# Attention, low-rank mix and feed-forward on one core: own buffers for the raw W2 chunks, W2 remainders on VectorE, and measured durations in the planner

## The chip, the core and the metric

The kernel runs on one core of one Trainium2 chip. The core has five instruction queues: TensorE (PE in the profile, its weight loads PEld), VectorE (DVE), ScalarE (ACT), GpSimd (POOL) and SyncE (SP, which only issues DMAs here). Each takes its instructions in order, and an instruction that waits for a semaphore holds all that stand behind it on the same engine. The metric is the device time of one execution in microseconds, the median of several runs.

## The reference

Eight batches, eight heads, 576 positions, 64 channels a head. Two attentions are added (one over positions averaged by four, one over a window of seven positions), then a low-rank mix along the sequence (rank 32), then a feed-forward net from 512 to 2048 and back. Cut to what matters:

```python
q_d, k_d, v_d = (x.reshape(B, H, 144, 4, D).mean(axis=3) for x in (q, k, v))
out_up = np.repeat(sm_attn(q_d, k_d, v_d), 4, axis=2)
mask = np.abs(pos[:, None] - pos[None, :]) < 4
scores = np.where(mask, scale * q @ k.transpose(0, 1, 3, 2), -1e9)
x = out_up + softmax(scores) @ v             # then heads side by side: (8, 576, 512)
u = x + (x.transpose(0, 2, 1) @ U @ V).transpose(0, 2, 1)
out = u + np.maximum(u @ w_ch1, 0.0) @ w_ch2  # 512x2048, 2048x512
```

U, V and the two weight matrices arrive as 64-bit floats.

## The kernel before

**Feed-forward.** It takes most of the time of TensorE. u is kept transposed, channels on the partitions. A step is one batch (8), one half t of its positions (2 x 288) and one block fc of 128 of the 2048 hidden channels (16): 256 steps. Every product is made from operands that are split into a high part (H) and a remainder (L), as three matmuls: high by high, high by remainder, remainder by high. So F1 of a step (line 891) is 4 x 3 matmuls of 128x128 by 288 into a PSUM buffer ps_h, of which there are two. ScalarE writes hH, its rectified high part (line 898), VectorE the remainder hL (line 899). F2 of the same step (line 914) comes three steps later (LAG = 3): four groups of three matmuls into four accumulators acc, which run over the 16 blocks of a half. At the end of a half GpSimd adds uH and uL (line 924), VectorE adds that to each accumulator (line 928), and SyncE stores the result (line 931). Steps are counted from 0; step 32 is the first of batch 1.

**Attention and mix.** They work on two heads at a time, a head pair hp (four to a batch). Batch 0 goes through a way of its own (the "early" functions), with buffers in a pool named early. Batches 1 to 7 go through late_global, late_scores, local_attn and mix_part: q and k are loaded (gq, gT, line 570), GpSimd averages them (gh, smq, smk) and v (vr, vs, lines 511 and 513); TensorE makes both kinds of scores (ps_b, lines 718 and 725), ScalarE copies the local ones (se), SyncE stores them to a scratch in DRAM (s_s, line 751) and loads them back in another layout (sc, line 757). The global attention ends with ps_t (line 540), ps_a (line 553), od (VectorE, line 557) and four stores up_s (line 562). In the local attention, GpSimd multiplies the window of v with the weights (Pt, line 798, five pieces to a pair, three buffers), VectorE sums them (acc, line 803), SyncE stores the sum (x_s, line 805). It is loaded back as xL and Y (lines 821 to 832) for the mix: GpSimd takes the remainder of xL (line 839), TensorE multiplies with U (ps_hu, line 847) and V (ps_u, line 862), VectorE adds (xT, line 865), ScalarE writes uH (line 868) and GpSimd uL (line 870). Then the pair is ready for F1. The attention of batch b + 1 is planned beside the feed-forward of batch b.

**Weights.** W1 and W2 come as 16 chunks each of 512 KB (lines 390 and 398) into raw buffers. Three slots, which later serve as the products Pt of the local attention, hold all raw chunks in turn. A chunk is converted (convert, lines 336 to 351): ScalarE brings out the upper bits (upper, line 339), VectorE joins them with the lower ones (c, line 342), ScalarE writes the high part (W1H or W2H, line 346), GpSimd the remainder (W1L or W2L, line 349). W2H and W2L lie where the early pool was, so that their writes wait for the key "late", which the last operation of batch 0's attention sets; the loads of W2 do not wait for it. F1 waits for it as well from step 3 on.

**What sets the order.** Nothing is written out by hand. Every operation is put into a Plan with its engine, an estimate of its duration, what it reads and writes, and a priority. Plan.run (line 104) is a list scheduler that simulates the five engines with these estimates, and the order that comes out is the program's. The helpers dve, act and pool_tt (lines 270 to 277) turn a number of elements and a base or a rate into a duration. The matmuls of the feed-forward have the lowest priority (FILL) and so fill what the attention leaves free; hH, hL and the output adds have the highest (FIRST). So a changed estimate can move any instruction on any engine.

The three places where the estimates enter:

```python
return op(DVE, ((n / 2 if two_x else n) + 65) / 960.0, fn, r, w, prio)
return op(ACT, n / 1200.0 + base, fn, r, w, prio)
return op(POOL, 0.147 + n * ns / 1000.0, fn, r, w, prio, after)
```

## Time and profile before

| what | us |
|---|---|
| median of three runs | 980.32 |
| the three runs | 980.32, 982.18, 973.27 |
| the profiled execution | 982.36 |
| its span in the profile | 980.6 |

The profile is of one execution. Its page gives the busy time of each engine; further views give it by stretches of time, the chain of waits that ended last, the timeline of each engine, and groups of instructions by line. In a row of a timeline stand the start, the duration (both in us), the engine, the line of the kernel, the operation, its output and inputs, and in brackets how long the engine was idle ahead of it and what ended that. The mean granted clock of TensorE is 0.975 of full speed. By the page, 120.19 MB were moved by DMA, at a mean of 123 GB/s.

### The profile page before, as it was taken

The numbers are of one execution on the slowest core, as the hardware profiler recorded it, in microseconds if no ns is written. First come the engines' busy times: TensorE is split into PE (matmuls) and PEld (weight loads), VectorE is DVE, ScalarE is ACT, GpSimd is POOL, SyncE is SP. The second block draws the span as 40 slices with busy tenths as digits, with TensorE's granted clock in tenths as the row PEclk, the third lists the DMA queues.
The fourth block names the chain that finished last, engine by engine and source line by source line (L and its number), as shares of the span: only waits on it lengthen the run. The fifth ranks groups of instructions, "written<-read, shape, count | busy, mean of one in ns | idle before, by whom it ended". The sixth has DMA issues, their size and how long they took to land.

```text
span 980.6 us, 26568 instructions
## 1 busy us (share of the span) xinstructions
PE 928.4 (95%) x10712; PEld 907.5 (93%) x10712; DVE 475.3 (48%) x948; ACT 391.0 (40%) x1239; POOL 555.2 (57%) x591
## 2 busy tenths in 40 slices
PE   5878999859999999999999999999999999999998
PEld 4667989849999999999999999999999999999998
DVE  4554576544455655543555555544555544532122
ACT  3677653433344333443344334443344344221111
POOL 6786677766665746574656656565566646431010
PEclk9788999959999999999999999999999999999999
DMA  9858855655555455546555455545536454310000
GB/s 249 214 192 220 237 150 138 145 124 129 126 139 120 111 120 110 147 88 149 124 123 126 106 126 119 136 104 143 127 97 143 110 124 84 88 37 25 1 25 25
DMA packets 222930, 120.19 MB, mean 123 GB/s; under 512 B 174724, under 2 KB 199128, under 8 KB 222808
## 3 DMA queue, kind: packets, MB, share of 16 engines
q1 hardware_dynamic: 222808, 118.51, 49.7%
q8 instruction: 84, 1.38, 0.6%
q14 instruction: 38, 0.31, 0.1%
HBM read 87.60 MB, written 30.86 MB: 121 GB/s over the span
## 4 chain that ended last, share of the span: by engine, by line
PE 81%; DVE 7%; DMA 3%; issue 3%; ACT 3%; POOL 2%; SPq 1%; DVEq 0%; POOLq 0%; ACTq 0%
PE ps_h L891 35%; PE acc L914 34%; PE ps_a L553 3%; DVE acc L803 3%; PE ps_b L718 2%; PE ps_hu L847 1%; PE ps_t L540 1%; PE ps_b L725 1%; DVE o L928 1%; DVE c L342 1%; DMA kd<-in_kT 1%; POOL W2L L349 1%; PE ps_u L862 1%; PE ps_hu L666 1%; DMA w2r<-in_W 1%
## 5 line engine op out<-in xcount | busy, mean ns | idle before, releaser
L891 PE MATMUL ps_h<-uH,W1H 128*128 128x288 f32 x1024 | 298.2, 291 | 5.8 <-DVE hL L899 5.8
L914 PE MATMUL acc<-hH,W2H 128*128 128x288 f32 x1024 | 300.6, 294 | 2.5 <-ACT W2H L346 2.5
L891 PE MATMUL ps_h<-uL,W1H 128*128 128x288 f32 x1024 | 294.8, 288 | 0.0
L891 PE MATMUL ps_h<-uH,W1L 128*128 128x288 f32 x1024 | 294.7, 288 | 0.0
L914 PE MATMUL acc<-hH,W2L 128*128 128x288 f32 x1024 | 294.2, 287 | 0.5 <-POOL W2L L349 0.5
L914 PE MATMUL acc<-hL,W2H 128*128 128x288 f32 x1024 | 294.0, 287 | 0.0
L798 POOL TENSOR_TENSOR Pt<-vl,at 128x896 f32<-128x896 f32 (+1 forms) x140 | 227.0, 1690 | 108.1 <-DVE acc L803 53.4
L899 DVE SCALAR_TENSOR_TENSOR hL<-ps_h,hH 128x288 fp32r<-128x288 f32 x256 | 116.5, 455 | 331.7 <-ACT hH L898 328.2
L898 ACT ACTIVATE hH<-ps_h 128x288 fp32r<-128x288 f32 x256 | 104.7, 409 | 343.8 <-PE ps_h L891 340.7
L891 PEld LDWEIGHTS ps_h<-uH,W1H 128*128 128x128 f32 x1024 | 195.6, 191 | 8.7 <-DVE hL L899 7.6
L914 PEld LDWEIGHTS acc<-hH,W2H 128*128 128x128 f32 x1024 | 194.6, 190 | 3.0 <-ACT W2H L346 2.6
L891 PEld LDWEIGHTS ps_h<-uL,W1H 128*128 128x128 f32 x1024 | 195.6, 191 | 0.0
L914 PEld LDWEIGHTS acc<-hH,W2L 128*128 128x128 f32 x1024 | 194.6, 190 | 0.9 <-POOL W2L L349 0.9
L891 PEld LDWEIGHTS ps_h<-uH,W1L 128*128 128x128 f32 x1024 | 195.4, 191 | 0.0
L914 PEld LDWEIGHTS acc<-hL,W2H 128*128 128x128 f32 x1024 | 194.7, 190 | 0.0
L803 DVE TENSOR_REDUCE acc<-Pt 128x128 f32<-128x1024 f32 (+1 forms) x140 | 151.5, 1104 | 2.6 <-POOL Pt L798 1.5
L839 POOL TENSOR_TENSOR xL<-xL,xH 116x640 fp32r<-116x640 f32 x28 | 43.3, 1545 | 105.8 <-ACT xH L838 93.4
L743 ACT ACTIVATE se<-ps_b 96x114 f32<-96x114 f32 x112 | 39.8, 355 | 77.3 <-PE ps_b L718 56.2
L924 POOL TENSOR_TENSOR o<-uH,uL 128x288 f32<-128x288 f32 x48 | 36.9, 797 | 50.4 <-DMA out_t<-o 50.4
L511 POOL TENSOR_TENSOR vr<-vr 72x256 f32<-72x256 f32 x56 | 40.8, 729 | 36.5 <-DMA vr<-in_v 36.5
L792 ACT ACTIVATE Pt<-ul 128x128 f32<-128x128 f32 (+1 forms) x140 | 48.5, 422 | 25.3 <-DVE acc L803 21.5
L870 POOL TENSOR_TENSOR uL<-xT,uH 128x288 fp32r<-128x288 f32 x56 | 43.7, 801 | 22.0 <-ACT uH L868 22.0
(130 smaller groups left out, 1043.7 us busy)
## 6 DMA issues: line engine op xcount, KB each, us to landing
vl<-in_vp SPq DMA_DIRECT2D x56, 240.0 KB
w1r<-in_W SPq DMA_DIRECT2D x16, 511.8 KB
w2r<-in_W SPq DMA_DIRECT2D x16, 511.8 KB
gT<-in_kT SPq DMA_DIRECT2D x28, 291.0 KB
gq<-in_qT SPq DMA_DIRECT2D x28, 288.0 KB
vr<-in_v SPq DMA_DIRECT2D x56, 144.0 KB
up_s<-od SPq DMA_DIRECT2D x112, 72.0 KB
ul<-up_s SPq DMA_DIRECT2D x28, 288.0 KB
```

Of the source, the lines that this page charges most:

```text
L511: pool_tt(256, lambda x=x: nc.gpsimd.tensor_tensor(out=x()[:, :, 0:2, :], in0=x()[:, :, 0:2, :], in1=x()[:, :, 2:4, :], op=ALU.add), [x], ...
L743: act(n * KL, lambda p=ps[hh], se=se, n=n, rows=rows: nc.scalar.activation(se()[rows, 0:n].rearrange("p r k -> p (r k)"), p()[rows, 0:n * ...
L792: act(n * D, lambda n=n, ps=ps, Pt=Pt: nc.scalar.activation(Pt()[:, :n, :, 7], ul()[:, ps, :], AF.Copy), [ul], [(Pt, 1)], prio, 0.16)
L798: nc.gpsimd.tensor_tensor(out=Pt()[:, :n, :, 0:7].rearrange("p s d o -> p o s d"), in0=win, in1=at()[:, ps, :].rearrange("p s o -> p o s") ...
L803: dve(8.5 * n * D, lambda n=n, ps=ps, Pt=Pt: nc.vector.tensor_reduce(out=acc()[:, ps, :], in_=Pt()[:, :n], axis=AX.X, op=ALU.add), [(Pt, 0 ...
L839: pool_tt(640, lambda: nc.gpsimd.tensor_tensor(out=xL(), in0=xL().bitcast(F32), in1=xH().bitcast(F32), op=ALU.subtract), [xL, xH], [xL], prio)
L870: pool_tt(TN, lambda uH=uH, uL=uL, uf=uf: nc.gpsimd.tensor_tensor(out=uL()[:, hp, :], in0=uf(), in1=uH()[:, hp, :].bitcast(F32), op=ALU.su ...
L891: nc.tensor.matmul(ps()[:, :TN], w[:, dc, fs], turns(u()[:, dc, :]), start=(n == 0), stop=(n == 3 * NDC - 1))
L898: last_h[i] = act(TN, lambda: nc.scalar.activation(hH(), ps()[:, :TN], AF.Relu), [ps], [hH], FIRST, 0.05)
L899: dve(TN, lambda: nc.vector.scalar_tensor_tensor(hL(), ps()[:, :TN], 0.0, hH().bitcast(F32), op0=ALU.max, op1=ALU.subtract), [ps, hH], [hL ...
L914: nc.tensor.matmul(ac[e]()[:, :TN], W2[w][:, fc, es], turns(hx()), start=(fc == 0 and n == 0), stop=(fc == NFC - 1 and n == 2))
L924: pool_tt(TN, lambda e=e, o1=o1: nc.gpsimd.tensor_tensor(out=o1()[:, :TN].bitcast(F32), in0=uH()[:, e, :].bitcast(F32), in1=uL()[:, e, :]. ...
```

## The change

It has three parts.

1. Raw chunks 0 to 11 of W2 get four buffers of their own, in a pool "raws" that is laid into the space of the early pool once batch 0's attention has ended. Chunks 12 to 15 stay in the three shared slots. The converted chunks 0 to 11 lie in a tile W2a beside the raw buffers; when all of them are converted, the raw buffers are given up and chunks 12 to 15 are converted into a tile W2b in their place. High part and remainder lie side by side in both. So the load of chunks 0 to 11 now waits for "late"; the load of chunk f of the last four waits for the high part of chunk f - 4, and its conversion for a key "last".

2. The remainder of every W2 chunk is taken by VectorE instead of GpSimd (16 instructions of 128x512). W1, U and V stay on GpSimd.

3. Some forty estimates of durations are replaced.

No instruction is added or removed, and none but the 16 remainders changes its engine. The diff's core, with some of the estimates:

```diff
+class Later:
+    def __init__(self):
+        self.pool = None
+
+    def tile(self, *a, **k):
+        return self.pool.tile(*a, **k)
...
+    NFA = 12
...
+    first = tc.tile_pool(name="raws", bufs=1)
+    raws = Later()
+
     def late_pool():
-        if not W2:
-            early.__exit__(None, None, None)
-            w2p = ctx.enter_context(tc.tile_pool(name="w2p", bufs=1))
-            W2["H"] = w2p.tile([128, NFC, DM], F32R, name="W2H")
-            W2["L"] = w2p.tile([128, NFC, DM], F32R, name="W2L")
-        return W2
+        early.__exit__(None, None, None)
+        w2p = ctx.enter_context(tc.tile_pool(name="w2a", bufs=1))
+        W2["a"] = w2p.tile([128, NFA, 2, DM], F32R, name="W2a")
+        raws.pool = first.__enter__()
+
+    def last_pool():
+        first.__exit__(None, None, None)
+        w2p = ctx.enter_context(tc.tile_pool(name="w2b", bufs=1))
+        W2["b"] = w2p.tile([128, NFC - NFA, 2, DM], F32R, name="W2b")
+
+    def w2(f, i):
+        return W2["a"][:, f, i] if f < NFA else W2["b"][:, f - NFA, i]
...
-    def convert(raw, pp, n, hi_out, lo_out, a, wkey, name, prio, gate=(), l0=0):
+    def convert(raw, pp, n, hi_out, lo_out, a, wkey, name, prio, gate=(), l0=0, rest=POOL):
...
-        dve(1.2 * n, lambda: nc.vector.scalar_tensor_tensor(
+        dve(1.75 * n, lambda: nc.vector.scalar_tensor_tensor(
...
-        pool_tt(1.0 * n, lambda: nc.gpsimd.tensor_tensor(
+        eng, put = (nc.vector, dve) if rest == DVE else (nc.gpsimd, pool_tt)
+        put(1.25 * n if rest == DVE else 1.08 * n, lambda: eng.tensor_tensor(
             out=lo_out(), in0=ta()[l0:], in1=hi_out()[l0:].bitcast(F32), op=ALU.subtract),
...
     def load_w2(f, prio):
-        raw = raw_buf("w2r")
-        dma(lambda: nc.sync.dma_start(out=shifted(raw, 128, CN), in_=w2.bitcast(I16)[f * 128:(f + 1) * 128, 1:]),
-            [], [raw], prio, 525)
-        convert(raw, 128, CN, lambda: W2["H"][:, f, :].unsqueeze(1),
-                lambda: W2["L"][:, f, :].unsqueeze(1), 1, f"W2_{f}", "c2", prio, ["late"])
-
+        key, gate = f"W2_{f}", "late" if f < NFA else "last"
+        own = f < NFA
+        raw = buf(raws, [128, 2 * CN], I32, "w2r", None, 4) if own else raw_buf("w2r")
+        dma(lambda: nc.sync.dma_start(out=shifted(raw, 128, CN), in_=w2_in.bitcast(I16)[f * 128:(f + 1) * 128, 1:]),
+            [gate] if own else [f"W2_{f - 4}H"] if f >= NFA else [], [raw], prio, 525)
+        convert(raw, 128, CN, lambda: w2(f, 0).unsqueeze(1), lambda: w2(f, 1).unsqueeze(1), 1, key, "c2", prio,
+                [gate], rest=DVE)
...
-            pool_tt(7 * n * D, prod, [vl, at], [(Pt, 0)], prio, 1.75)
+            pool_tt(7 * n * D, prod, [vl, at], [(Pt, 0)], prio, 1.9)
...
-        last_h[i] = act(TN, lambda: nc.scalar.activation(hH(), ps()[:, :TN], AF.Relu), [ps], [hH], FIRST, 0.05)
-        dve(TN, lambda: nc.vector.scalar_tensor_tensor(
+        last_h[i] = act(TN, lambda: nc.scalar.activation(hH(), ps()[:, :TN], AF.Relu), [ps], [hH], FIRST, 0.17)
+        dve(TN + 82, lambda: nc.vector.scalar_tensor_tensor(
...
+    begun = len(plan.ops)
     for f in range(NFC):
+        if f == NFA:
+            plan.op(DVE, 0.0, lambda: last_pool(), [], ["last"], 27, after=plan.ops[begun:], lat=0.0)
         load_w2(f, W2P + W2S * f)
```

How the order moves is shown at three places. Line numbers of the changed kernel are 18 to 20 higher (390 becomes 409, 891 becomes 911, 914 becomes 934). A number behind x says how many like instructions follow one another.

SyncE's issues around the end of batch 0's attention; w1r and w2r are raw chunks, gq and gT the q and k of batch 1's first head pair, s_s its stores of scores. Before:

```order
L390 DMA w1r<-in_W 128x2047 x3
L509 DMA vr<-in_v 72x2x256
L390 DMA w1r<-in_W 128x2047 x3
L570 DMA gq<-in_qT 128x576
L570 DMA gT<-in_kT 128x582
L751 DMA s_s<-se 32x3x38 x3
L751 DMA s_s<-se 32x9x38
L751 DMA s_s<-se 32x3x38 x3
L751 DMA s_s<-se 32x9x38
L390 DMA w1r<-in_W 128x2047
L398 DMA w2r<-in_W 128x2047
```

The same place now:

```order
L409 DMA w1r<-in_W 128x2047 x8
L590 DMA gq<-in_qT 128x576
L419 DMA w2r<-in_W 128x2047 x4
L771 DMA s_s<-se 32x3x38 x3
L771 DMA s_s<-se 32x9x38
L771 DMA s_s<-se 32x3x38 x3
L771 DMA s_s<-se 32x9x38
L590 DMA gT<-in_kT 128x582
L419 DMA w2r<-in_W 128x2047 x3
```

The last chunk of W1 and the first four of W2 now stand ahead of the eight stores of scores; gT stands behind them.

TensorE at the end of batch 0, from the last F2 group (acc) of step 31 on; ps_hu and ps_u belong to the mix of a head pair, the others to attention. Before:

```order
L914 MATMUL acc_2372<-hH,W2L 128x288
L847 MATMUL ps_hu<-xH,Ust 64x128 x5
L847 MATMUL ps_hu<-xL,Ust 64x128 x5
L862 MATMUL ps_u<-Vst,stk 128x288 x2
L553 MATMUL ps_a<-vs,E 72x64 x8
L725 MATMUL ps_b<-smk,smq 32x144 x4
L725 MATMUL ps_b<-smk,smq 8x144 x2
L718 MATMUL ps_b<-gT,gq 32x38 x30
L725 MATMUL ps_b<-smk,smq 32x144 x4
L725 MATMUL ps_b<-smk,smq 8x144 x2
L718 MATMUL ps_b<-gT,gq 32x38 x6
L540 MATMUL ps_t<-ident_sb,E 72x72 x8
```

Behind these stand, before and now, ps_hu and ps_u of head pair 3 and then F1 of step 32. Now:

```order
L934 MATMUL acc_2340<-hH,W2b 128x288
L573 MATMUL ps_a<-vs,E 72x64 x8
L745 MATMUL ps_b<-smk,smq 32x144 x4
L745 MATMUL ps_b<-smk,smq 8x144 x2
L738 MATMUL ps_b<-gT,gq 32x38 x30
L745 MATMUL ps_b<-smk,smq 32x144 x4
L745 MATMUL ps_b<-smk,smq 8x144 x2
L738 MATMUL ps_b<-gT,gq 32x38 x6
L560 MATMUL ps_t<-ident_sb,E 72x72 x8
L867 MATMUL ps_hu<-xH,Ust 64x128 x5
L867 MATMUL ps_hu<-xL,Ust 64x128 x5
L882 MATMUL ps_u<-Vst,stk 128x288 x2
```

ps_hu and ps_u of head pair 2 have gone from here: ps_hu now stands ahead of F2 of step 28, ps_u ahead of F2 of step 29. Those of pair 0 moved from F2 of step 21 to that of step 17, those of pair 1 from behind F1 of step 29 to behind F2 of step 23. On SyncE, at this place, gq, gT and four stores of scores have come ahead of the load of xL, and on VectorE the four output adds of line 928 stand ahead of the last three sums acc of head pair 3.

TensorE at the start of a later batch (step 96), where the third F1 group of the batch follows the second. Before:

```order
L891 MATMUL ps_h<-uH,W1L 128x288
L891 MATMUL ps_h<-uH,W1H 128x288
L891 MATMUL ps_h<-uL,W1H 128x288
L891 MATMUL ps_h<-uH,W1L 128x288
L553 MATMUL ps_a<-vs,E 72x64 x8
```

Now:

```order
L911 MATMUL ps_h<-uH,W1L 128x288
L573 MATMUL ps_a<-vs,E 72x64 x8
L911 MATMUL ps_h<-uH,W1H 128x288
L911 MATMUL ps_h<-uL,W1H 128x288
L911 MATMUL ps_h<-uH,W1L 128x288
```

ps_a has moved from behind the third group to between the second and the third. At the start of batch 2 (step 64), ps_a and a head pair's scores stand ahead of the first and the second group in the same way. Just ahead of these places, ps_u of head pair 3 has moved: before, it stands ahead of F2 of the third step from the end of the batch, now among the four groups of F2 of the last step. At the last batch (step 224) nothing stands between the first three F1 groups, before and now.

More of the change, by code (lines that the diff above doesn't have):

```diff
@@ L675, in early_mix @@
             [ph, (stk, 0)], [(stk, 1)], prio)
-        act(128, lambda: nc.scalar.activation(stk()[3 * R:4 * R], ph()[:R, :2 * D], AF.Copy), [ph], [(stk, 2)], prio, 0.1)
+        act(128, lambda: nc.scalar.activation(stk()[3 * R:4 * R], ph()[:R, :2 * D], AF.Copy), [ph], [(stk, 2)], prio, 0.16)
         for t in range(NT):
@@ L738, in mm @@
                 dense(3, r)
[L739 removed]
+        op(PE, 1.38, mm, [qr, kr, sq, sk, "early_hu"], ps, prio)
         for hh in range(2):
@@ L850, in mix_part @@
         stk = buf(mix, [128, 2, D], F32R, "stk", bufs=2)
-        act(128, lambda: nc.scalar.activation(stk()[0:2 * R], pv(), AF.Copy), [ph], [(stk, 0)], prio, 0.05)
+        act(128, lambda: nc.scalar.activation(stk()[0:2 * R], pv(), AF.Copy), [ph], [(stk, 0)], prio, 0.17)
         dve(128, lambda: nc.vector.tensor_tensor(
@@ L854, in mix_part @@
             [ph, (stk, 0)], [(stk, 1)], prio)
-        act(128, lambda: nc.scalar.activation(stk()[3 * R:4 * R], pv()[0:R], AF.Copy), [ph], [(stk, 2)], prio, 0.05)
+        act(128, lambda: nc.scalar.activation(stk()[3 * R:4 * R], pv()[0:R], AF.Copy), [ph], [(stk, 2)], prio, 0.17)
         for t in range(NT):
```

81 lines of the change are left out of this document (40 added, 41 removed).

## The prediction, made before the changed kernel was run

> **What bounds the kernel now.** I read the first part of the page, then the busy time by stretches of time, then the chain of waits where those show a hole, then the timelines of single engines there.
>
> From the page, the busy time of the engines (share of the span, instructions):
>
> ```profile
> PE 928.4 (95%) x10712; PEld 907.5 (93%) x10712; DVE 475.3 (48%) x948; ACT 391.0 (40%) x1239; POOL 555.2 (57%) x591
> ```
>
> TensorE is the bound on average: 980.6 us of span less 928.4 leaves 52.2 us that can be won without taking matmuls away. Where they lie is told by TensorE's busy time by stretches: first one whole batch (111.5 us, the next four are alike), then all engines in 25 us stretches.
>
> ```profile
> 328.50:440.00 111.50, 110.58 (x1299) 1.00 0.52 122
> ```
> ```profile
> 75.00:100.00 25.00, 20.45 (x246) 19.17 (x245) 12.07 (x26) 18.52 (x52) 17.09 (x19) 0.86 0.85 218
> ...
> 175.00:200.00 25.00, 19.46 (x163) 18.82 (x163) 15.47 (x30) 8.05 (x23) 20.17 (x21) 0.97 0.49 111
> 200.00:225.00 25.00, 16.20 (x176) 14.40 (x177) 11.74 (x21) 9.71 (x32) 16.59 (x19) 0.55 0.60 135
> 225.00:250.00 25.00, 25.00 (x305) 24.79 (x305) 11.01 (x22) 10.02 (x34) 15.29 (x17) 1.00 0.52 117
> ```
>
> (Columns: length, busy PE, PEld, DVE, ACT, POOL, granted clock, DMA share, GB/s.) From 225 us on TensorE is never idle for long: 0.94 us in each batch. The holes are before that: 4.55 us at 75 to 100 and 5.54 + 8.80 = 14.3 us at 175 to 225, where the clock also falls to 0.55. The first is the start of the second matmul, the other the change from batch 0 to batch 1. So the change can act at three places: the start, that one boundary, and the 0.94 us per batch.
>
> **The start (chunks of W2).** TensorE's row where the second matmul first runs, SyncE's issues ahead of it, then the conversions on VectorE and GpSimd, grouped by line:
>
> ```profile
> 86.67 0.61 PE L914 MATMUL acc<-hH,W2H 128*128 128x288 f32 x1 [2.47 <-ACT W2H L346]
> ```
> ```profile
> 63.51 6.42 SPq L390 DMA_DIRECT2D w1r<-in_W  x3
> 72.04 0.33 SPq L570 DMA_DIRECT2D gq<-in_qT  x1
> ...
> 72.90 4.33 SPq L751 DMA_DIRECT2D s_s<-se  x8
> 77.33 0.40 SPq L390 DMA_DIRECT2D w1r<-in_W  x1
> 78.48 0.35 SPq L398 DMA_DIRECT2D w2r<-in_W  x1
> ```
> ```profile
> L342 DVE SCALAR_TENSOR_TENSOR c<-w1r,upper x16: 653/867/2364, 25.5 to 82.6; 128x512 int32<-128x512 int32 x16
> L342 DVE SCALAR_TENSOR_TENSOR c<-w2r,upper x16: 675/961/1230, 84.8 to 133.8; 128x512 int32<-128x512 int32 x16
> ```
> ```profile
> L349 POOL TENSOR_TENSOR W2L<-c,W2H x16: 1270/1278/1714, 86.7 to 137.5; 128x512 fp32r<-128x512 f32 x16
> ```
> ```profile
> 70.96 0.80 POOL L699 TENSOR_TENSOR uL<-uf,uH 128x288 fp32r<-128x288 f32 x1
> 71.71 1.28 POOL L349 TENSOR_TENSOR W1L<-c,W1H 128x512 fp32r<-128x512 f32 x1
> ```
> ```profile
> 71.33 2.22 DVE L342 SCALAR_TENSOR_TENSOR c<-w1r,upper 128x512 int32<-128x512 int32 x1 [1.39 <-issue]
> ```
>
> Step by step. The first W2 load is issued at 78.48 and its product starts at 86.67: 8.19 us from issue to use. In the old order it stands behind eight stores of scores (4.33 us) and the sixteenth W1 load. In the new one all W1 loads and one gq load come first, four W2 loads follow, the stores come after. Two things can hold the new load: the gate "late", open when the last work of batch 0's attention ends (uL at 70.96 + 0.80 = 71.76), so with gq's 0.33 an issue at about 72.4; or the sixteenth W1 load, which needs the slot of the thirteenth chunk, whose c ends at 71.33 + 2.22 = 73.55, then 0.40 for itself and 0.33 for gq: 74.3. Adding 8.19 gives 80.6 or 82.5; I take the middle, 81.6, which is 5 us earlier. Ends: 6.1 us of gain; against it, three more W1 conversions now stand ahead of the first hL on VectorE, 3 x 0.867 = 2.6 us of loss if nothing covers them. What covers them now is the time until the first F1 product is there; without it the 2.6 us falls due.
>
> Moved behind the four W2 loads (about 4 x 0.35 = 1.4 us, more if the slots are late) are the stores of scores of batch 1's first head pair. I cost that at nothing on the path, since F1 of batch 1, for which that chain works, is 145 us away; without that cover it is 1.4 us.
>
> Remainders on VectorE: no row of before has this one there. The nearest is c, same 128x512 and also two inputs in SBUF: 0.675 alone, 0.961 in the middle, 1.230 at worst. I take 0.961: 16 x 0.961 = 15.4 us more for VectorE, hidden in a stretch where it is half idle (12.07 of 25 us busy), and 16 x 1.278 = 20.4 us less for GpSimd. On the path to F2.0 lies one of them: 0.3 us won, contained in the middle I took. If VectorE were blocked for as long as c was at worst, 2.364, a remainder would cost 1.1 us against 1.278 and F2.0 came at 82.7.
>
> The trace shows VectorE's c stretched from 0.653 to 2.364 us when GpSimd works beside it. The Trainium skill, "SBUF — State Buffer", section "SBUF: two separate sides", has a rule that speaks against this move: a VectorE operation with two inputs in SBUF and a GpSimd operation that reads SBUF take the shared ports as an exclusive lock, and the one that comes second waits for the whole of the other. By it each remainder on VectorE gives back up to 0.675 us of the 1.278 that GpSimd is spared, so GpSimd would win 16 x 0.603 = 9.6 us rather than 20.4, and F2.0 would wait for one more GpSimd operation of 1.28 us: a start term of -3.7 in place of -5, a sum 1.3 us higher. The stretched rows agree with the rule; how often the two meet in the new order no row tells.
>
> **The boundary from batch 0 to batch 1.** The chain of waits there (three of its pieces), TensorE's timeline, then SyncE's and VectorE's:
>
> ```profile
> 188.39 4.42 PE acc L914 x36
> ...
> 208.36 0.47 SPq L821
> ...
> 217.34 6.92 PE ps_h L891 x36
> ```
> ```profile
> 192.64 0.47 PE L847 MATMUL ps_hu<-xH,Ust 116*64 116x128 f32 x5
> ...
> 213.07 0.80 PE L847 MATMUL ps_hu<-xH,Ust 116*64 116x128 f32 x5 [1.47 <-ACT xH L838]
> ```
> ```profile
> 201.91 0.33 SPq L805 DMA_DIRECT2D x_s<-acc  x1
> 203.13 0.34 SPq L509 DMA_DIRECT2D vr<-in_v  x1
> 204.87 3.38 SPq L562 DMA_DIRECT2D up_s<-od  x4
> 208.36 0.47 SPq L821 DMA_DIRECT2D xL<-x_s  x1
> ...
> 211.49 1.86 SPq L751 DMA_DIRECT2D s_s<-se  x4
> ...
> 215.85 0.40 SPq L570 DMA_DIRECT2D gq<-in_qT  x1
> 216.30 0.42 SPq L570 DMA_DIRECT2D gT<-in_kT  x1
> ```
> ```profile
> 193.54 0.64 DVE L928 TENSOR_TENSOR upper<-acc,upper 128x288 f32<-128x288 f32 x1
> ...
> 198.22 1.22 DVE L803 TENSOR_REDUCE acc<-Pt 128x128 f32<-128x1024 f32 x1
> ```
>
> Call the end of batch 0's half with step 31 T: 188.39 + 4.42 = 192.8. F1 of batch 1 (step 32) starts at 217.34, T + 24.5; it waits for head pair 3, whose sums are stored at 201.91 (T + 9.1), queue behind up_s, and from the reload at 208.36 take 8.98 us to F1. In the new order the sums (hu) of head pair 2 no longer stand in this hole but four steps earlier. VectorE has four output adds and three sums left behind T: 4 x 0.64 + 3 x 1.22 = 6.2, the store is issued at T + 6.2. Ahead of the reload on SyncE then stand the store 0.33, vr 0.34, up_s 3.38, gq and gT 0.82 and four stores of scores 1.86, 6.7 together: reload at T + 12.9, F1 at T + 21.9. That is 2.6 us sooner. This is an edit that removes and adds: 9.1 - 6.2 = 2.9 us won ahead of the store, the scores' stores and gq, gT added on SyncE. Bounds: if three of the four adds are done before T, as the old order has them, 1.9 us more (-4.5); if the chain is set by the distance of head pairs alone, -7.4 (below); on the other side the new items of SyncE on top of the old times, +2.7.
>
> **The later boundaries.** TensorE's waits between 300 and 900 us, and from the chain a filler's length:
>
> ```profile
> PE ps_h L891 <- DVE hL L899: 4.7, 5, 1.0
> ```
> ```profile
> 225.74 1.03 PE ps_a L553 x16
> ```
>
> Five times, at a batch's start, the third F1 group waits 0.94 us for a buffer that hL still reads. In the new order ps_a (1.03 us) stands between the second and third group: five waits filled, 5 x 0.94 = -4.7 us. Its price is that the matmuls of head pair 3 (ps_u) move from 4 us ahead of the batch's first F1 to right ahead of it, 1.1 us of matmuls between. How long the path from ps_u to uL takes, TensorE's and GpSimd's rows for pair 2 of batch 1 show:
>
> ```profile
> 185.03 0.43 PE L862 MATMUL ps_u<-Vst,stk 128*128 128x288 f32 x2
> ```
> ```profile
> 186.37 0.80 POOL L870 TENSOR_TENSOR uL<-xT,uH 128x288 fp32r<-128x288 f32 x1 [2.33 <-ACT uH L868]
> ```
>
> That is 187.17 - 185.03 = 2.14 us. Covered are 1.1 us of matmuls and three quarters of the first F1 group (1.1 of 1.47 us), since it reads head pair 3 last: 2.2. So I cost the move at nothing; what comes later than that TensorE waits for, at each of six boundaries.
>
> Sum, on the profiled execution (982.36 us): -5 - 2.6 - 4.7 = -12.3, so 970.1. The median of the runs is 980.32, 2.04 lower: 968.
>
> **Rivals.**
> A, as summed: 968, own range 962 (start -6.1, boundary -7.4, and 4.7) to 975 (start nothing).
> B, batch 1's attention chain sets the time of F1.32, whenever F2 starts: the waits between 175 and 225 are all for that chain, so an earlier start only lengthens them. The sums of pairs 0 and 1, too, stand four or five steps earlier among TensorE's instructions, which run in order: if the chain isn't earlier by as much, TensorE waits there, and has the wait of the boundary sooner. Then both first terms vanish and 980.32 - 4.7 = 975.6 is left. For it: TensorE is idle 14.3 us there while GpSimd is 20.17 of 25 us busy; against it: GpSimd loses 20.4 us of work before that.
> C, the boundary follows the distance of head pairs: hu of pair 2 at 192.64 and of pair 3 at 213.07 are 20.4 us apart. Pair 2's now stands 7.6 us ahead of T (five groups of 1.47 and a ps_u of 0.26), so pair 3's falls at T + 12.8 and F1, 4.27 us after it, at T + 17.1: -7.4 in place of -2.6, 963. For it: those distances are the chain's own; against: the queue of SyncE just counted.
> D, slower: head pair 3 arrives just too late at every boundary. The place is GpSimd's uL between two products Pt, rows of the page:
>
> ```profile
> L798 POOL TENSOR_TENSOR Pt<-vl,at 128x896 f32<-128x896 f32 (+1 forms) x140 | 227.0, 1690 | 108.1 <-DVE acc L803 53.4
> L511 POOL TENSOR_TENSOR vr<-vr 72x256 f32<-72x256 f32 x56 | 40.8, 729 | 36.5 <-DMA vr<-in_v 36.5
> ```
>
> With two Pt and one vr ahead of it, 2 x 1.69 + 0.73 = 4.1 us, on top of the 2.14 us that the 2.2 us just cover, each of six boundaries loses 4.0: +24, which makes 968 into 992. It decides from 2 us of lateness on (6 x 2 = 12, the whole gain). For it: the order has no slack left there; against: GpSimd is a third idle late in the run (57% busy).
>
> **How the numbers follow.** About 1%, 9.8 us, is what a measurement of this kernel can tell from no change. A 0.45, B 0.25, C 0.15, D 0.15. The time is A's. The range leaves out D and little else: low 958 (C with the best start is 962; the 2.5 us that the first three F1 groups lose to the low clock, 6.92 against 3 x 1.47, and the 1.9 of the adds take it there), high 983 (B with the boundary 2.7 us worse, and one Pt late at some boundaries). Faster by over 1% is below 970.5: C whole and about 0.28 of A's 0.45: 0.43. Within 1%: the rest of A and B: 0.42. Slower: D, 0.15.
>
> **What would show it.** Start right: the first second-matmul row at 80 to 83 us; wrong: at 86 or later. Boundary right: F1 of batch 1 some 22 us after T, and the clock still low there; C: 17; B: F1 at 217 whatever T is. Later right: 110.5 us a batch in place of 111.4, and no wait for hL; D: waits of F1 for uL at six boundaries. Remainders: 0.7 to 1.2 us on VectorE, and GpSimd busy some 20 us less. What would make all of it wrong is a new wait on VectorE between 80 and 140 us, where conversions, remainders and hL now share one queue.

## The result, and the profile after

The changed kernel takes 990.74 us, the median of four runs (989.33 to 992.37). The kernel before took 976.80 us beside it (four runs, 972.62 to 982.18). The ratio is 1.0142, 95% interval 1.0097 to 1.0186: slower by some 14 us, where 12 us less was forecast.

The profiled executions are closer: 989.67 us (span 987.8) after, 982.36 us (span 980.6) before. A second profile of the kernel before, taken in the study, gave 982.74 us and the same times of its steps within 0.5 us from step 17 on, while the medians of its timed runs lay between 976.80 and 980.38. So a profile of the kernel before lies 2 to 6 us above the medians of its timed runs; why, no run told. Below, ratios come from timed runs, and the profiles are used for places.

The page of the changed kernel, busy time by engine:

```profile
PE 933.2 (94%) x10712; PEld 912.3 (92%) x10712; DVE 482.1 (49%) x964; ACT 387.6 (39%) x1239; POOL 538.2 (54%) x575
```

GpSimd lost 17.0 us and VectorE gained 6.8. The 16 remainders take 14.2 us on VectorE, while its conversions c became 4.7 us shorter and its operations ms and at of the attention 3.1. Twelve of the remainders (shortest, middle and longest in ns):

```profile
L368 DVE TENSOR_TENSOR W2a<-c,W2a x12: 675/684/2094, 82.4 to 113.4; 128x512 fp32r<-128x512 f32 x12
```

TensorE is busy 4.8 us longer with the same 10712 matmuls, at a mean granted clock of 0.965 instead of 0.975.

Where the time went is told best by a clock made of steps: the start of hH on ScalarE, minus the same in the kernel before (first profile), for the changed kernel and for some of the experiments below. A number that grows from one column to the next is time lost there, or work of the attention that one order has there and the other elsewhere.

| kernel | step 4 | 17 | 18 | 32 | 63 | 64 | 128 | 223 | 224 | 255 |
|---|---|---|---|---|---|---|---|---|---|---|
| before, us | 90.83 | 142.09 | 145.03 | 220.41 | 325.42 | 332.62 | 555.42 | 876.78 | 883.64 | 971.78 |
| changed | -5.6 | -7.5 | +1.3 | +1.2 | +1.5 | +8.3 | +6.5 | +5.6 | +7.7 | +7.7 |
| durations alone | -8.0 | -8.7 | -10.1 | -5.0 | -6.1 | -2.4 | -3.4 | -4.2 | -2.1 | -2.1 |
| raw buffers alone | -0.8 | -4.2 | -1.8 | -0.9 | -1.7 | +2.0 | +2.0 | +2.0 | +2.0 | +2.0 |
| changed, ms later | -6.8 | -9.4 | -6.0 | -3.3 | -3.4 | +3.5 | +1.7 | +0.9 | +3.1 | +3.1 |
| changed, slack x 0.75 | -6.5 | -5.8 | -5.7 | -2.6 | +1.4 | -3.2 | -4.6 | -7.7 | -11.6 | -8.6 |

Read along the second row, the changed kernel wins 7.5 us by step 17, loses 8.8 in the one step from 17 to 18, holds that over the boundary to batch 1, loses 6.8 from step 63 to 64 (5.0 of it still there at step 128), gains back about 0.4 at the start of each later batch (it stands at +5.7 at step 192), and loses 2.1 at step 224. The three losses are three places. They turn the -7.5 us of step 17 into +7.7 at step 255; the timed runs differ by 14 us, and the rest of that has no place in these profiles.

**Start.** TensorE's timeline of the changed kernel, the first row of the second matmul:

```profile
82.28 0.36 PE L934 MATMUL acc<-hH,W2a 128*128 128x288 f32 x1
```

It ran at 86.67 before: 4.4 us sooner. SyncE issues the four W2 loads behind gq, as the order said; below are GpSimd's last uL of batch 0:

```profile
73.74 0.33 SPq L590 DMA_DIRECT2D gq<-in_qT  x1
74.27 2.94 SPq L419 DMA_DIRECT2D w2r<-in_W  x4
```
```profile
72.23 2.02 POOL L719 TENSOR_TENSOR uL<-uf,uH 128x288 fp32r<-128x288 f32 x2
```

They end at 72.23 + 2.02 = 74.25, and that opens the gate "late": the loads go out at 74.27.

**Step 17 to 18.** TensorE's one large wait there, then VectorE, then GpSimd at the same time:

```profile
141.24 0.46 PE L745 MATMUL ps_b<-smk,smq 64*32 64x144 f32 x5 [3.81 <-DVE od L577]
```
```profile
135.37 5.49 DVE L789 SCALAR_TENSOR_TENSOR ms<-sc,mask_sb 128x63 f32<-128x63 f32 x1
140.78 0.41 DVE L577 TENSOR_TENSOR od<-ps_a,ri 72x256 f32<-72x256 f32 x1
```
```profile
135.02 0.73 POOL L531 TENSOR_TENSOR vr<-vr 72x256 f32<-72x256 f32 x1
135.71 5.15 POOL L818 TENSOR_TENSOR Pt<-vl,at 128x896 f32<-128x896 f32 x3
```

ms has 63 elements a partition. The other 27 of this trace took 0.22 us in the middle and 0.55 at most; here it takes 5.49, until 140.86, which is the end of GpSimd's third Pt (135.71 + 5.15). od stands behind it on VectorE, and the scores on TensorE wait for od. The clock falls with the wait (0.86 in this stretch; columns as in the prediction):

```profile
125.00:150.00 25.00, 20.69 (x243) 19.88 (x242) 20.75 (x26) 11.09 (x37) 19.12 (x19) 0.86 0.59 146
...
175.00:200.00 25.00, 22.80 (x278) 21.80 (x276) 12.80 (x23) 10.17 (x34) 18.78 (x22) 0.95 0.51 124
200.00:225.00 25.00, 12.48 (x143) 10.98 (x143) 10.20 (x22) 9.20 (x32) 15.12 (x16) 0.50 0.54 123
```

**Boundary to batch 1.** The last two rows are its hole: 2.20 + 12.52 = 14.7 us idle, against 14.3 before. TensorE's rows there:

```profile
195.14 0.29 PE L934 MATMUL acc<-hH,W2b 128*128 128x288 f32 x1
...
206.55 1.41 PE L560 MATMUL ps_t<-ident_sb,E 72*72 72x72 f32 x8 [3.40 <-ACT E L546]
213.33 0.79 PE L867 MATMUL ps_hu<-xH,Ust 116*64 116x128 f32 x5 [5.37 <-ACT xH L858]
...
217.40 0.44 PE L911 MATMUL ps_h<-uH,W1H 128*128 128x288 f32 x1
```

The end T of batch 0 is 195.14 + 0.29 = 195.4, and F1 of batch 1 follows at T + 22.0. Before, T was 192.8 and the same row stood at 217.13, T + 24.3 (the chain gives 217.34). Two rows of SyncE, the store of pair 3's sums and its reload, give the pieces:

```profile
199.90 0.33 SPq L825 DMA_DIRECT2D x_s<-acc  x1
207.52 0.47 SPq L841 DMA_DIRECT2D xL<-x_s  x1
```

The store goes out at T + 4.5, the reload at T + 12.1, and F1 comes 9.9 us after it.

**Step 64.** TensorE, and what VectorE does while TensorE waits for stk:

```profile
331.65 0.29 PE L934 MATMUL acc<-hH,W2b 128*128 128x288 f32 x1
334.22 0.82 PE L882 MATMUL ps_u<-Vst,stk 128*128 128x288 f32 x2 [2.29 <-DVE stk L872]
335.75 2.18 PE L573 MATMUL ps_a<-vs,E 72*72 72x64 f32 x16 [0.70 <-DVE xT L885]
337.69 0.59 PE L911 MATMUL ps_h<-uH,W1H 128*128 128x288 f32 x1
```
```profile
331.45 1.21 DVE L823 TENSOR_REDUCE acc<-Pt 128x128 f32<-128x1024 f32 x1
332.58 0.63 DVE L948 TENSOR_TENSOR o<-acc,o 128x288 f32<-128x288 f32 x1
333.12 0.64 DVE L948 TENSOR_TENSOR upper<-acc,upper 128x288 f32<-128x288 f32 x1
333.79 0.28 DVE L872 TENSOR_TENSOR stk<-ps_hu,stk 32x128 fp32r<-32x128 f32 x1
334.11 1.22 DVE L823 TENSOR_REDUCE acc<-Pt 128x128 f32<-128x1024 f32 x1
335.25 0.81 DVE L885 TENSOR_TENSOR xT<-ps_u,xT 128x288 f32<-128x288 f32 x2
```

stk and xT belong to head pair 3, which F1 of the new batch needs; each stands behind a sum of 1.2 us or behind output adds that only become possible when the half ends. The waits are 2.29 + 0.70 = 2.99 us, and in this kernel the granted clock falls with them. Five microseconds at a time, all engines:

```profile
325.00:330.00 5.00, 5.00 (x43) 5.00 (x42) 3.20 (x4) 2.53 (x8) 3.11 (x4) 1.00 0.30 38
330.00:335.00 5.00, 2.71 (x23) 2.22 (x21) 4.74 (x8) 0.85 (x3) 4.50 (x6) 0.92 0.32 111
335.00:340.00 5.00, 4.30 (x27) 4.25 (x27) 3.74 (x11) 1.27 (x4) 2.46 (x4) 0.50 0.69 194
340.00:345.00 5.00, 5.00 (x121) 4.58 (x121) 1.28 (x3) 2.24 (x7) 5.00 (x4) 0.90 0.51 119
```

Half clock for 5 us and 0.92 and 0.90 beside it cost 5 x (0.08 + 0.50 + 0.10) = 3.4 us more; 6.4 in all. The kernel before idled 0.92 us at this place (4.08 of 5 us busy) with the clock at 1.00 throughout. The difference, 5.5 us, is about the 5.0 that stay. The clock doesn't fall with every such wait: two of the parts alone, below, have the wait without it.

**Step 224, and the waits for hL.** TensorE's waits of the changed kernel between 300 and 900 us:

```profile
PE ps_u L882 <- DVE stk L872: 2.7, 2, 2.3
PE ps_h L911 <- DVE hL L919: 0.9, 4, 0.2
PE ps_a L573 <- DVE xT L885: 0.7, 1, 0.7
PE ps_h L911 <- POOL uL L890: 0.5, 1, 0.5
PE ps_h L911 <- ACT uH L888: 0.5, 1, 0.5
```

The wait for hL fell from 0.94 to 0.23 us, as planned. The short waits for stk (the second of them), uH and uL are step 224, where pair 3 is late as well and nothing else stands beside it: 0.39, 0.47 and 0.48 us, on VectorE, ScalarE and GpSimd.

### The profile page after: what moved, and what is told of

It is laid out like the page before. It is cut to its first block, busy times and chain, and to the rows that moved or that the text cites. A ratio compares the mean times of both kernels' runs of the same rounds, so it can differ in the third digit from the quotient of the medians.

```text
span 987.8 us, 26473 instructions
## 1 busy us (share of the span) xinstructions
PE 933.2 (94%) x10712; PEld 912.3 (92%) x10712; DVE 482.1 (49%) x964; ACT 387.6 (39%) x1239; POOL 538.2 (54%) x575
## 4 chain that ended last, share of the span: by engine, by line
PE 81%; DMA 9%; DVE 4%; ACT 3%; issue 1%; POOL 1%; SPq 1%; DVEq 0%; ACTq 0%; POOLq 0%
PE acc L934 36%; PE ps_h L911 35%; DMA w1r<-in_W 3%; PE ps_a L573 2%; PE ps_b L738 2%; DMA w2r<-in_W 2%; PE ps_hu L867 2%; DVE acc L823 1%; PE ps_b L745 1%; PE ps_t L560 1%; ACT upper L357 1%; DMA s_s<-se 1%; DMA qt<-in_qT 1%; DVE o L948 1%; PE ps_u L882 1%
## 5 line engine op out<-in xcount | busy, mean ns | idle before, releaser
L934 PE MATMUL acc<-hH,W2a 128*128 128x288 f32 x1536 | 323.5, 290 | 0.5 <-DVE W2a L368 0.4
L934 PEld LDWEIGHTS acc<-hH,W2a 128*128 128x128 f32 x1536 | 254.2, 190 | 1.7 <-DVE W2a L368 0.6
L934 PE MATMUL acc<-hL,W2a 128*128 128x288 f32 x768 | 220.1, 287 | 0.0
L934 PEld LDWEIGHTS acc<-hL,W2a 128*128 128x128 f32 x768 | 145.7, 190 | 0.0
L934 PE MATMUL acc<-hH,W2b 128*128 128x288 f32 x512 | 106.1, 289 | 0.0
L934 PEld LDWEIGHTS acc<-hH,W2b 128*128 128x128 f32 x512 | 84.3, 189 | 0.0
L934 PE MATMUL acc<-hL,W2b 128*128 128x288 f32 x256 | 73.3, 286 | 0.0
```

Source lines behind the costliest of these rows:

```text
L934: nc.tensor.matmul(ac[e]()[:, :TN], w2(fc, w)[:, es], turns(hx()), start=(fc == 0 and n == 0), stop=(fc == NFC - 1 and n == 2))
```

## The experiments

**The parts one by one.** Each is the kernel before with one part of the change, except the fourth, the changed kernel without its second part.

New durations alone (part 3, some forty estimates as in the changed kernel):

```diff
-        dve(1.2 * n, lambda: nc.vector.scalar_tensor_tensor(
+        dve(1.75 * n, lambda: nc.vector.scalar_tensor_tensor(
...
-            pool_tt(7 * n * D, prod, [vl, at], [(Pt, 0)], prio, 1.75)
+            pool_tt(7 * n * D, prod, [vl, at], [(Pt, 0)], prio, 1.9)
```

> Only the new durations; W2 chunks loaded and converted as before (shared slots, remainders on GpSimd). Theory O (the loss is the order that the new durations make: head pair 3 late at the boundaries, loads of pair 3 behind stores on SyncE): F2 starts at 86 us or later as before, ps_u of pair 3 stands right ahead of steps 64 and 224 as in the changed kernel, and the time is at or above that of the kernel before, 982 to 995 us. Rival V (the loss is VectorE's new remainders, held up by GpSimd): no such hold, 965 to 978 us. Rival L (the loss is that W2's loads now wait for the end of batch 0's attention): 965 to 978 us.

981.05 us, ratio 1.0022 (1.0003 to 1.0041): just below the range of O, above that of V and L. O was wrong on the start, which is better than in the whole change: F2 starts at 79.36 (-8.0 at step 4). ms isn't held for more than 1.61 us, and there is no jump at step 18 (3.9 us go by step 20). The losses at steps 64 (+3.7) and 224 (+2.1) are there, as O has it. TensorE at step 64, and all engines there:

```profile
326.72 0.50 PE L872 MATMUL ps_u<-Vst,stk 128*128 128x288 f32 x2 [2.34 <-DVE stk L862]
```
```profile
325.00:330.00 5.00, 2.28 (x14) 1.89 (x15) 4.94 (x8) 1.54 (x4) 3.88 (x4) 1.00 0.24 84
330.00:335.00 5.00, 5.00 (x115) 4.83 (x117) 3.77 (x12) 1.70 (x5) 2.57 (x4) 1.00 0.69 195
```

The wait for stk is as long as in the changed kernel, and TensorE idles 2.7 us of the first stretch, yet the granted clock stays at 1.00. So this step loses 3.7 us here and 6.8 there.

Raw buffers alone (part 1):

> Only the own raw buffers and the gates of the W2 loads; durations as before, remainders on GpSimd. Theory O: ps_u of pair 3 stands four steps ahead of step 96 on as before, no wait over 1 us at steps 96 to 224; one at step 64, where hu and ps_u stand behind F2 of step 63; 970 to 985 us. Rival L: the loss is here, 985 to 995 us. Rival V: no loss, 965 to 978 us.

982.59 us, ratio 1.0042 (1.0020 to 1.0063), as O expects. F2 starts at 82.97; the own buffers bring 0.8 us by step 4 and 4.2 by step 17, and the time is worse. From step 63 to 64 it loses 3.7 us, at the same wait:

```profile
331.02 0.50 PE L881 MATMUL ps_u<-Vst,stk 128*128 128x288 f32 x2 [2.37 <-DVE stk L871]
```

The clock stays at 1.00 here too. So either part puts ps_u of pair 3 where stk comes too late for step 64, the raw buffers with the old durations as well; the loss at step 224 comes with the durations only.

Remainders on VectorE alone (part 2):

```diff
+        eng, put = (nc.vector, dve) if rest == DVE else (nc.gpsimd, pool_tt)
-        pool_tt(1.0 * n, lambda: nc.gpsimd.tensor_tensor(
+        put(1.0 * n, lambda: eng.tensor_tensor(
```

> Only the W2 remainders on VectorE; durations and loads as before. Theory O: 16 rows of about 0.7 us on VectorE, now and then over 2 us beside GpSimd, and the time within 1% of the kernel before, 968 to 985 us. Rival V: waits of TensorE behind held VectorE operations between 90 and 150 us, 985 to 995 us. Rival L: no loss, 965 to 980 us.

977.48 us, ratio 0.9975 (0.9958 to 0.9991): a small gain, in the range of O and of L.

The whole change, remainders back on GpSimd:

```diff
-                [gate], rest=DVE)
+                [gate])
```

> The changed kernel with the W2 remainders on GpSimd again (durations and raw buffers stay). Theory O: the order at steps 64 and 224 is the changed kernel's, so the loss stays, 985 to 995 us. Rival V: the loss goes with the remainders, 965 to 980 us. Rival L: it stays, 985 to 995 us.

982.63 us, ratio 1.0043 (1.0023 to 1.0064): below what O and L expect, above V. At step 18 it loses 2.6 us instead of 8.8 (-9.0 at step 17, -6.4 at 18) and stands at -6.1 at step 32, 7.3 us ahead of the changed kernel; the loss at step 64 is unchanged (-6.4 to +0.4). ms is held for 2.01 us at most in it. So the parts alone give +0.2, +0.4 and -0.25%, and together +1.4%: they don't add. Each moves the whole order, and places where two things meet, as ms and three products, appear and vanish.

**Undoing the three losses by hand.** These take the changed kernel's order and move a few instructions in it; the plan stays. ms of pair 2 of batch 1 behind the instructions up to its own lmx on VectorE, so that od passes it:

```diff
+MOVES = [
+    ((DVE, (1, 2), "ms", 0), (DVE, (1, 2), "lmx", 0)),
+]
...
+        for o, y in [(find(*what), find(*ahead_of)) for what, ahead_of in MOVES]:
+            order.remove(o)
+            order.insert(order.index(y), o)
```

> The changed kernel with one VectorE instruction moved: the first operation ms of pair 2 of batch 1 (line 789, held for 5.49 us at 135.37 while GpSimd ran three products back to back) now stands behind od and the output adds, ahead of lmx. If the port that VectorE and GpSimd share holds it: od runs at 135.4, TensorE's wait of 3.81 us at 141.24 is gone, steps 18 to 31 come 4 to 9 us sooner, T falls near 188; whatever then stands first with two inputs in SBUF is stretched instead. If F1 of step 32 is set by pair 3's attention alone, it comes at 217 as before and the time stays within 2 us (988 to 992); if the lost steps also held pair 3, it is 3 to 6 us sooner (984 to 987). If ms was slow by itself (its load late), nothing changes.

986.67 us, ratio 1.0092 (1.0073 to 1.0110), in the range expected if the lost steps also held pair 3. od runs at 133.73, the wait of 3.81 us is gone, and F1 of step 32 comes at 212.85, 4.5 us sooner, though T falls only to 191.3 and not near 188. A third of the loss of the change is back (0.5 of 1.42%; the two intervals just overlap, but the clock of steps has the same, 4.6 us at step 255). ms is held again where it now stands, with less behind it. VectorE and GpSimd of this kernel:

```profile
138.79 4.45 DVE L802 SCALAR_TENSOR_TENSOR ms<-sc,mask_sb 128x63 f32<-128x63 f32 x1
```
```profile
135.59 5.27 POOL L831 TENSOR_TENSOR Pt<-vl,at 128x896 f32<-128x896 f32 x3
140.72 1.53 POOL L872 TENSOR_TENSOR xL<-xL,xH 116x640 fp32r<-116x640 f32 x1
142.22 0.99 POOL L831 TENSOR_TENSOR Pt<-vl,at 128x448 f32<-128x448 f32 x1
```

On SyncE, at the boundary to batch 1, the loads ul, xL and Y of pair 3 ahead of scores' stores and of gq of later pairs:

```diff
+    ((SP, (1, 3), "ul", 0), (SP, (2, 0), "s_s", 0)),
+    ((SP, (1, 3), "xL", 0), (SP, (2, 2), "gq", 0)),
+    ((SP, (1, 3), "Y", 0), (SP, (2, 2), "gq", 0)),
```

> The changed kernel with three of SyncE's issues moved, all of pair 3 of batch 1: the load ul ahead of the eight stores of scores of batch 2's first pair, and xL and Y ahead of gq, gT and the stores of scores of its second pair. Theory O: xL goes out at 204.6 or sooner instead of 207.5, F1 of step 32 comes 3 to 5 us sooner, the time falls to 985 to 988. Rival: something else (the sums behind the output adds, the low clock) sets F1 of step 32: no change, 989 to 992.

988.77 us, ratio 1.0106 (1.0083 to 1.0128): between theory and rival. F1 of step 32 comes 1.7 us earlier (215.66), not 3 to 5, with T all but unchanged (195.18).

On VectorE, at step 64, two output adds (o1) and two sums moved behind stk and xT of pair 3, and the stores of the output with them:

```diff
+    ((DVE, ("f", 66), "o1", 2), (DVE, (3, 0), "acc", 4)),
+    ((DVE, ("f", 66), "o1", 3), (DVE, (3, 0), "acc", 4)),
+    ((DVE, (3, 0), "acc", 2), (DVE, (3, 0), "acc", 4)),
+    ((DVE, (3, 0), "acc", 3), (DVE, (3, 0), "acc", 4)),
...
```

> The changed kernel with the boundary from batch 1 to 2 put right: on VectorE two sums of the next batch's pair 0 (acc) and the last two output adds now stand behind stk and xT of pair 3, and the two stores of these adds behind that on SyncE. Theory O: TensorE's wait of 2.29 us ahead of ps_u at 334 falls under 0.6, the clock stays up, F1 of step 64 starts 3 to 5 us sooner, and the time falls by as much: 985 to 987. Rival: pair 3 of batch 2 is late for another reason (its uL on GpSimd): under 1.5 us.

990.02 us, ratio 1.0113 (1.0098 to 1.0129): the gain that theory O expects didn't come. The wait for stk fell from 2.29 to 0.26 us; then ps_a waits 0.42 for xT and 0.81 for GpSimd's vs. From step 63 to 64 it still loses 4.7 us instead of 6.8, and the granted clock falls as in the changed kernel, with 1.5 us of idle time in place of 3.0:

```profile
335.00:340.00 5.00, 5.00 (x110) 4.72 (x108) 3.63 (x10) 0.88 (x3) 2.42 (x3) 0.50 0.69 206
```

So the attention is late on more than one engine, and how long TensorE waits doesn't say what the clock adds.

All three:

> The three edits together. Theory O: they lie on one path one behind the other, so the gains add: 7 to 14 us below the changed kernel, 976 to 983. Rival: the attention chain takes up what the first two win, only the third is left: 985 to 988.

985.72 us, ratio 1.0075 (1.0052 to 1.0099), in the range of the rival: the gains add only in part, and half of the loss remains.

**The planner's slack.** The same estimates hold one number that the change left as it was. A DMA of high priority (80 and up, which is the attention of batches 2 and later) is taken to land 3 us later than its size says if it reads something computed, 4 us if not; a middle one half of that. The longer this slack, the later the plan puts what uses the load. The changed kernel with the slack shortened:

```diff
-        late = (3.0 if r else 4.0) * (0.5 * (prio >= 50) + 0.5 * (prio >= 80))
+        late = (3.0 if r else 4.0) * (0.5 * (prio >= 50) + 0.5 * (prio >= 80)) * 0.75
```

> The changed kernel with one more number of the planner changed: the slack that it adds to each load and store of the late attention (3 or 4 us, half of it for batch 1) is taken three quarters. Theory O (the engines' durations were raised to what was measured while the slack on DMAs stayed, so the planned chain of pair 3 became longer than the real one and its place fell behind the end of the batch): in the new order ps_u of pair 3 stands steps ahead of steps 64 and 224, so the waits there (2.29 and 0.70 at 334, the three of 0.39 to 0.48 at 888) are gone: 8 to 10 us below the changed kernel, 979 to 984. Rival: the real chain is as long as planned: then TensorE waits for pair 3 at its new, earlier places, and the time stays at 988 or above.

971.24 us beside 979.73, ratio 0.9911 (0.9879 to 0.9943): faster than both kernels, and by more than theory O expects. From 300 us on, no wait of TensorE is listed. In the changed kernel ps_u of pair 3 of batch 2 runs at 334.22, 6.7 us ahead of hH of step 64 (340.95); here it runs at 311.56, 17.8 us ahead (329.40). TensorE's row in this kernel, then its busy time in one batch, and the same stretch in the changed kernel:

```profile
311.56 0.43 PE L882 MATMUL ps_u<-Vst,stk 128*128 128x288 f32 x2
```
```profile
330.50:442.00 111.50, 111.50 (x1318) 1.00 0.57 131
```
```profile
330.50:442.00 111.50, 108.51 (x1258) 0.97 0.52 122
```

TensorE is busy all of it at full clock. The hold of ms is still there in this kernel (5.33 us at 136.33, step 17 to 20: -5.8 to +1.5).

Half the slack:

> As the run before with half of the slack. Theory O: a little lower again or the same, 974 to 984. Rival: with less slack than the loads take, TensorE waits in the middle of the batches, 985 or above.

972.60 us, ratio 0.9924 (0.9902 to 0.9947): the same as with three quarters, within the intervals.

The kernel before with the slack x 0.75:

> The kernel before, old durations, with three quarters of the slack. If the slack matters only beside the raised durations, no more than the five waits of 0.95 us can be won: 972 to 980. If less slack is good by itself, the gain is as large as in the changed kernel, 968 to 972. If the old durations need the slack (their sum stood in for it), TensorE waits for pair 3: 984 or above.

Ratio 0.9996 (0.9976 to 1.0016). With the old durations and the shared raw slots the shorter slack does nothing measurable. The raw buffers with the old durations, which lose at step 64 too, weren't run with it.

The changed kernel with the shorter slack, and ms of pair 2 of batch 1, with its lmx, moved to just ahead of that pair's second ms:

> The kernel of d7_loads_sooner with ms and lmx of pair 2 of batch 1 moved behind od, the output adds and three sums on VectorE. If the hold is on the path there too: the wait of 3.00 us at 142.66 goes and the time falls by 2 to 4 us, 967 to 969. If F1 of step 32 is set by pair 3 alone: no change, 970 to 973.

970.11 us, ratio 0.9903 (0.9883 to 0.9924): no difference from 0.9911, as expected if pair 3 alone sets F1 of step 32. No profile of it shows the place.

The changed kernel with the shorter slack, remainders on GpSimd:

> The kernel of d7_loads_sooner with the W2 remainders on GpSimd. If the remainders on VectorE are a loss of their own (as the changed kernel against e4_gpsimd_rest, 0.8%): 963 to 968. If that loss was one held operation at a bad place: within 3 us, 968 to 975. If they are a gain: 976 or above.

970.03 us, ratio 0.9907 (0.9887 to 0.9928). With this slack, where the remainders run can't be told in the time. With the old one it makes 1% (1.0142 and 1.0043), and that stands in the steps up to 32.

The new durations with the shorter slack, without raw buffers and with the remainders on GpSimd:

> The kernel before with the new durations alone and the planner's DMA slack times 0.75: raw W2 chunks in the three shared slots, remainders on GpSimd. Theory (the new durations and the slack belong together, and the raw buffers and remainders add little): the holes that the durations alone have at steps 64 and 224 (3.7 and 2.1 us) go, as they did in the changed kernel, and the time comes out 5.8 us below that of the durations alone, ratio 0.994 to 0.998, with most of what the changed kernel with the shorter slack won. Rival (the gain of the shorter slack needs the raw buffers, which let the start and the boundary of batch 1 move): the holes stay or others open, ratio 1.000 to 1.004. If it comes out at 0.991 or less, the raw buffers and remainders give nothing at all.

976.71 us beside 979.56, ratio 0.9960 (0.9935 to 0.9985), as the theory expects: TensorE doesn't wait after 300 us, and steps 63 to 64 cost 0.4 us instead of 3.7. The whole change with this slack (0.9911) is better still. The run just above (0.9907, 0.9887 to 0.9928) differs from this one by the raw buffers alone, and the two intervals don't meet, if only just: beside the new durations and the shorter slack the raw buffers give some 5 us, where alone they cost 0.4%.

**What holds ms.** Two small kernels measure it by itself; they compute nothing of the reference.

> A kernel of its own that computes nothing of the reference and writes zeros. GpSimd runs n products without a pause (the first 128x512, the others 128x896; n is 0, 1, 2, 4, 8), and beside them VectorE runs a reduction and then the operation ms of the local attention (128x63, two inputs in SBUF); then n = 4 with a reduction of 63 elements in place of ms (one input), and with ms reading one input from PSUM. If the whole run of GpSimd's products holds ms: ms takes some 0.2 us at n = 0 and then ends with GpSimd's last product, about 0.6, 2.3, 5.7 and 12 us for n = 1, 2, 4, 8; the reduction and the one from PSUM take 0.2 us. If only the product under way holds it: no more than about 1.7 us, whatever n. If ms was slow for another reason: 0.2 us throughout.

VectorE's rows of this kernel: the operation with two inputs in SBUF with no product, then with two and with eight products back to back on GpSimd; a sum with one input beside four; and the operation with one of its inputs in PSUM beside four.

```profile
3.39 0.22 DVE L58 SCALAR_TENSOR_TENSOR two_a<-sc,m 128x63 f32<-128x63 f32 x1
...
7.44 0.79 DVE L58 SCALAR_TENSOR_TENSOR two_a<-sc,m 128x63 f32<-128x63 f32 x1
...
19.57 0.78 DVE L58 SCALAR_TENSOR_TENSOR two_a<-sc,m 128x63 f32<-128x63 f32 x1
...
35.77 0.21 DVE L63 TENSOR_REDUCE one_b<-sc 128x9 f32<-128x63 f32 x1
...
43.86 0.21 DVE L58 SCALAR_TENSOR_TENSOR two_c<-ones,m 128x63 f32<-128x63 f32 x1
```

It is held until the product that is under way ends (the first, of 1.26 us), and no longer.

> A kernel of its own that computes nothing of the reference and writes zeros. Eleven times GpSimd runs four products without a pause (the first 128x512, 1.26 us, then three of 128x896), and the operation ms (two inputs in SBUF) comes on VectorE behind a reduction whose length grows, so that it arrives from 0.2 to 1.4 us after the first product's start. If the time of arrival decides: early ones end with the first product, those that arrive in its last 0.4 us are held through a second one or through all (up to 7 us). If the kind of product decides (the kernel's Pt reads a window and a broadcast, these don't): all end with the product under way.

With the moment of arrival moved through the first product of 1.26 us and into the second of 2.07, eleven times, it took between 0.21 and 2.08 us. It ended within 0.1 us of the end of the product under way, or, where it came just as one ended, ran in 0.21 us. So neither the number of these products nor the moment explains 5.49 us. The kind of product doesn't either: with half the slack, ms was held as long over plain additions and a subtraction, which read no window. VectorE and GpSimd of that kernel:

```profile
192.69 3.54 DVE L789 SCALAR_TENSOR_TENSOR ms<-sc,mask_sb 128x63 f32<-128x63 f32 x1
```
```profile
192.32 2.30 POOL L944 TENSOR_TENSOR o<-uH,uL 128x288 f32<-128x288 f32 x3
194.58 0.81 POOL L944 TENSOR_TENSOR upper<-uH,uL 128x288 f32<-128x288 f32 x1
195.34 0.80 POOL L890 TENSOR_TENSOR uL<-xT,uH 128x288 fp32r<-128x288 f32 x1
```

**The kernel before once more**, for the profile named above:

> The kernel before, unchanged, for a second profile. If its executions differ at the boundary from batch 0 to 1 (a hold or a DMA there), F1 of step 32 starts up to 5 us sooner than 217.3; if they differ evenly, every stage is shorter by the same share.

982.74 us, the same order and, from step 17 on, the same times of steps within 0.5 us.

## Why the prediction was wrong

By the clock of steps the forecast of -12.3 us became +7.7. Of these 20 us, 8.8 lie ahead of step 32 (forecast -5 - 2.6, measured +1.2), 7 to 9 at steps 64 and 224, and some 3 in the later waits.

- **The start** was right in size: -5 forecast, -4.4 at F2 and -5.6 at step 4 measured. F2 began at 82.28 (forecast 81.6, the later of its two bounds 82.5), with the W2 load issued at 74.27. That this is the later bound of 74.3 is luck: the bound came from the slot of the sixteenth W1 load, but all W1 loads were issued by 68.6, and what held the W2 loads was the gate "late", which opened at 74.25 and not at 71.76. Which part of the change does it wasn't asked: the new durations alone start F2 at 79.36, the raw buffers alone at 82.97.
- **Remainders on VectorE** were right: 0.68 us in the middle, 2.09 at worst, GpSimd 17 us less busy (forecast "some 20"). The Trainium skill's rule in "SBUF — State Buffer", section "SBUF: two separate sides", was to make the sum 1.3 us higher; the row of 2.09 agrees that a remainder can be held by a product, and the time of the two ways with the shorter slack, 971.24 and 970.03, shows no price.
- **VectorE between 80 and 140 us** is the first step that failed. The prediction named a new wait there as what would make all of it wrong, and put it into the sum at nothing. It came, at 135: ms, held while GpSimd ran, kept od back, TensorE waited 3.81 us, and the clock fell to 0.86 in that stretch. It isn't a conversion or a remainder that was held there but an operation of the attention that had stood elsewhere. Of the 8.8 us in that step, moving ms wins back 4.9 (0.5% of 979).
- **The boundary** came out as forecast, F1 at T + 22.0 (forecast T + 21.9), by two errors that nearly cancel: the store at T + 4.5 instead of T + 6.2, the reload at T + 12.1 instead of T + 12.9, and 9.9 us from there instead of 9.0. T itself was 2.6 us later, not 5 us sooner. But T doesn't set F1 in general: in the other kernels F1 follows T by 13.0 us (half the slack: T 199.5, F1 212.5) to 25.3 (new durations and shorter slack). Rival B, the attention chain sets F1 whenever T is, is nearer to that, though its 217, which the changed kernel has (217.40), is no rule either: with the durations alone F1 comes at 212.09. With SyncE's loads put first, F1 moved by 1.7 us, so the queue of SyncE that the term counted is part of it. Rival C's T + 17 wasn't reached.
- **The 0.94 us waits** went as forecast, to 0.23, but each is worth only about 0.4 us (+6.5 at step 128, +5.7 at 192, two batch starts on), and there are four of them now: 1.6 us, not 4.7.
- **The other step that failed** is "So I cost the move at nothing" of ps_u of head pair 3. It set 2.14 us of path, read off pair 2 of batch 1, against 2.2 us of cover, and began the path at ps_u. The 1.1 us of matmuls behind ps_u were read off step 96. At steps 96, 128, 160 and 192 nine of F2 do follow it, and there the cover holds: TensorE waits neither for stk nor for uL. At the two that lose, 64 and 224, ps_u stands behind the last F2 group (for step 64 the change's text has it among the groups), and no F2 follows. At step 64 ps_u itself is late by 2.29 us, because stk stands on VectorE behind output adds, and the half's end is just when those fall due; then xT stands behind a sum. The lower clock that followed added 3.4 us. Rival D had the mechanism (pair 3 too late) with 15%, but put it on GpSimd's uL at six boundaries of 4.0 us; it was two, 6.8 us at VectorE's stk and xT and 2.1 us at stk, uH and uL. That D's time of 992 is near the measured 990.74 is chance.
- **In the sums**, A's upper end of 975 ("start nothing") is 973 by its own terms, 968 + 5.

What was shown: the loss at step 64 comes with the new durations and with the raw buffers, each alone; the loss at 224 comes with the durations; both go with the shorter slack, in the changed kernel and with the durations alone, while the kernel before gains nothing from it. That the hold of ms is worth 4 to 5 us at step 32 and in the time is what moving it gives; with the shorter slack it is there too (5.33 us), and moving it changes nothing. Not shown: why ms is held over several instructions; when the clock falls with a wait; why the raw buffers alone move ps_u; and why the timed runs of some kernels differ by up to 6 us from what the profiles give.

## What to carry to other kernels

A list scheduler's estimates work together: when durations are replaced by measured ones, the slack that stood beside the old ones has to be tuned again (here 1.0142 became 0.9911), and the order's weak places (which pair is due when, and what stands ahead of it on each engine) have to be read out of the new order. The parts of such a change are to be timed one by one and together, since +0.2, +0.4 and -0.25% made +1.4%. A wait is not to be priced by its length alone: 3.0 us of waits on TensorE at step 64 cost 3.4 us more in clock, 1.5 us of them the same 3.4, and 3.3 and 3.5 us, in two other orders, nothing.
